# The rest columns of x of problem B, issued without a wait for the main transposing load

## The chip, the cores and the metric

The kernel runs on one core of one Trainium2 chip. The metric is device time in microseconds (us) of one execution. TensorE (PE) does the matmuls, VectorE (DVE) and ScalarE (ACT) move results out of the accumulators in PSUM, GpSimd (POOL) copies V, and SyncE (SP) does nothing but issue transfers (DMAs). ACT issues DMAs too. All transfers run on the same 16 DMA engines.

## The reference

Two independent problems, A and B, with inputs of the same shapes and no mask. Each one is a block of grouped-query attention over a given K and V cache, with the projection into Q before it and the output projection behind it. The two outputs stand side by side in the result.

```
x (16, 80, 576)   k_cache, v_cache (16, 16, 512, 128)   wq (576, 4096)   wo (4096, 576)   all bfloat16
q      = (x @ wq) as 16 x 32 heads x 80 x 128
k, v   = each of the 16 cached heads used by two query heads
p      = softmax(q k^T / sqrt(128))
out    = (p v, heads side by side) @ wo                          # 16 x 80 x 576
result = concatenate(out of A, out of B)                         # 16 x 80 x 1152
```

## The kernel before

**Units.** The work is cut into 128 units. A unit is one batch row and four cached heads: 512 keys by 128 channels for each of the four, 512 KB of K and 512 KB of V. Units 0 to 63 are problem A, units 64 to 127 problem B. Within a problem, 16 units (all batch rows) share four cached heads and so one block of 1024 columns of wq and 1024 rows of wo. Four units in a row share one block of 320 rows of x.

**What happens to a unit.** K comes from memory through a transposing DMA (`em_ldk`, L931) into `kT`, which has `NK` = 5 buffers, so unit U uses the buffer of unit U-5. The scores are matmuls of 160 columns (L898), 16 for each unit; ACT takes the exponential (L903) into `P`. V comes through a plain DMA (`em_ldv`, L935) into `v_in`; POOL copies it (L938) into `v_sb`, which has a column of ones for the row sums. P times V is L995 and L1011, the normalisation L1030 and L1035, the transposition of the result L1054, the output projection L1091. The projection of x into Q (L871) reads the transposed x in `xT` and is done in pieces between the other matmuls, some units ahead of its use.

**x.** `xT` holds the transposed x in `NX` = 5 slots of 320 rows. The 576 columns are five chunks of 128: four full ones, and a fifth made of the last 128 columns. Problem A's four blocks are loaded at the start and transposed on PE. Problem B's four blocks (numbers 4 to 7) come through transposing DMAs in the middle of the run: `em_ldx` (L807) brings columns 0 to 511 of a block, and `em_ldx2` (L810) the last 128, "the rest columns". Block 4 goes to slot 4, which was empty; blocks 5, 6 and 7 go to slots 0, 1 and 2, which held blocks of problem A. No projection of problem B reads them until it has waited for both landings.

**Order and waits.** Each operation is registered with `add(engine, key, ...)`. The key is a time in units of its own (16 for each unit); on each engine the operations are issued in the order of the keys, strictly one after the other, so an operation that waits holds up everything behind it on its engine. `_Sched.finalize` derives the waits: an operation that writes a named resource waits for its last writer and for all its readers since. The engine waits by a semaphore, and a DMA's semaphore counts when the data has landed. `xres(sl)` names the resources of problem A's block in slot `sl`; `em_ldx` lists them as written, so it waits until the last projection of A has read the slot.

**SP's queue.** SP issues all the K loads, half of the V loads (ACT has the other half), the loads of x, and nearly all stores of results (`out`, L1130). Problem B's x loads have keys that put them between K loads: block 4 ahead of the K load of unit 42, block 5 ahead of unit 52's, block 6 ahead of unit 56's, block 7 ahead of unit 60's, each with its L807 and L810 next to each other.

Of the kernel before, what the change touches and what calls it, by code (L numbers as in the profile page):

```python
# [618 lines left out]
def bass_concat_heads__gqa_block_cached__gqa_block_cached__near_ridge_kernel(  # L619
# [9 lines left out]
    B, SQ, D = A_x.shape  # L629
# [39 lines left out]
    xT = sb("xT", [128, 5, NX * QN], BF16)  # L669
# [27 lines left out]
    def R(res, ver):  # L697
        return (res, ver)
# [4 lines left out]
    def add(eng, key, emit, dur=0.0, after=None, **kw):  # L703
        op = S.add(eng, key + 1000.0, emit, **kw)
        if eng == "pe":
            pe_time.append((op, dur))
        if after is not None:
            follow.append((op, after))
        return op
# [60 lines left out]
    def xres(c):  # L770
        return [("xT", c, g, part) for g, n in XB[c] for part in range(n)]
# [29 lines left out]
    for xb in range(4, 8):  # L801
        c = xb - 4
        x_ap = probs[1][0].rearrange("b s d -> (b s) d")[c * QN:(c + 1) * QN, :]
        sl = xb % NX

        def em_ldx(e, x_ap=x_ap, sl=sl):
            return e.dma_start_transpose(xT[:, 0:4, sl * QN:(sl + 1) * QN], x_ap[:, 0:512].rearrange("n (c d) -> n c d", d=128))  # L807

        def em_ldx2(e, x_ap=x_ap, sl=sl):
            return e.dma_start_transpose(xT[:, 4, sl * QN:(sl + 1) * QN], x_ap[:, D - 128:D])  # L810

        t = 16.0 * (36, 46.5, 50, 54)[c] + 9.0
        add("sp", t, em_ldx, writes=[R(("xT", sl, "B", 0), xb)] + ([R(r_, xb) for r_ in xres(sl)] if sl < 4 else []),
            dsem="d_x%d" % sl, name="ldx%d" % xb)
        add("sp", t + 0.1, em_ldx2, writes=[R(("xT", sl, "B", 1), xb)] + ([R(r_, xb) for r_ in xres(sl)] if sl < 4 else []), dsem="d_x%d" % sl, name="ldx%db" % xb)

    for goct in range(2 * NOCT):
        prob, q = divmod(goct, NOCT)
        wq_ap, wo_ap = probs[prob][3][:, q * 1024:(q + 1) * 1024], probs[prob][4][q * 1024:(q + 1) * 1024, :]
        sl = goct % 2  # L820
        if goct == 0:
            for hf, (n0, n1) in enumerate(WQ0):
                def em_a(e, wq_ap=wq_ap, n0=n0, n1=n1):
# [3 lines left out]
                    dsem="d_wi%d" % hf, name="ldwa0.%d" % hf)  # L827
# [5 lines left out]
        else:  # L833
            for ck in range(5):
# [6 lines left out]
                if goct == 2:  # L841
                    wr += [R(("wi", hf), 1) for hf in range(4)] if ck == 0 else []
                add("act", 256.0 * (goct - 1) + 16.0 + 20.0 * ck if goct > 1 else W1_T[ck], em_w,
                    writes=wr, dsem="d_wq%d" % sl, name="ldw%d.%d" % (goct, ck))
        for pc in range(4):
            def em_wo(e, wo_ap=wo_ap, sl=sl, pc=pc):
# [3 lines left out]
            t = 256.0 * goct - 56.0 + 22.0 * pc  # L850
            add("act", t if goct else WO_T[pc], em_wo, writes=[R(("wo", sl, pc), goct)], dsem="d_wo%d" % sl,
                name="ldwo%d.%d" % (goct, pc))

    for m in range(2 * NOCT * 4):
        goct, c = divmod(m, 4)
        prob = goct // NOCT
        wsl, qsl, xb = goct % 2, m % NQ, prob * 4 + c
        xsl = xb % NX
        for i in range(8):
            g, s_ = divmod(i, 2)  # L860
            t = 64.0 * m - 88.0 + 8.0 * i + 3.3
            if m == 0:
                t = -96.0 + 2.0 * i
            if 0 < m < 8:
                t = Q_T[m - 1][0] + Q_T[m - 1][1] * i
# [57 lines left out]
    for U in range(NSU):  # L923
# [21 lines left out]
        if U < NKP:  # L945
# [8 lines left out]
            def em_ldy(e, kc_ap=kc_ap, b=b, q=q, kin=kin):  # L954
# [3 lines left out]
                name="ldy%d" % U)  # L958
# [20 lines left out]
    def tmain(W, k):  # L979
        return 64.0 * W + T_PV0 + T_PV1 * k  # L980
# [5 lines left out]
    for W in range(NW):  # L986
        for k in range(16):
# [4 lines left out]
            def em_pv(e, g=g, bank=bank, off=off, vps=vps, U=U):  # L992
# [8 lines left out]
                writes=[R(("ps", bank), ("O", F))], name="pv%d.%d" % (U, g), dur=0.228)  # L1001

        def em_pr(e, W=W):
# [15 lines left out]
            writes=[R(("ps", PVB[(7 * W + 5) % 2]), ("O", 7 * W + 5)), R(("ps", PVB[(7 * W + 6) % 2]), ("O", 7 * W + 6))],  # L1019
            name="pr%d" % W, dur=1.12)  # L1020

        for f in range(7):
# [9 lines left out]
            def em_nrm(e, bank=bank, nt=nt, c0=c0, osl=osl):  # L1032
# [7 lines left out]
                writes=[R(("o", osl), F)], name="nrm%d" % F, after=(tn, sub + 0.1, 0.0))  # L1040

        for u in range(5):
# [3 lines left out]
            t = (tmain(W, 3 * lastf + 2) if lastf < 5 else 64.0 * W + T_PR + 4.0) + (9.5 if u < 3 else 7.5) + (1.5 if u == 4 else 0.0)  # L1046
# [27 lines left out]
    for h8 in range(NH8):  # L1074
# [3 lines left out]
        for n in range(10):  # L1078
            ti, ch = divmod(n, 2)
            r = 5 * hb + ti  # L1080
            t = (128.0 * h8 + 66.0 + 12.8 * n if h8 else OP_T[0] + OP_T[1] * n)
            if h8 == NH8 - 1:
                t = 64.0 * (NW - 1) + LAST_T[n]
# [53 lines left out]
    for k, (key, _, emit, reads, name, ver, evac) in enumerate(jobs):  # L1137
        bank = JB[k % 3]
        jo = add("pe", key, lambda e, emit=emit, bank=bank: emit(e, bank), reads=reads, writes=[R(("ps", bank), ver)],
                 name=name, dur={"qp": 0.68, "op": 0.98, "tr": 0.228, "tk": 0.228, "tx": 0.28}[name[:2]])  # L1140
        for eng, ek, em, rd, wr, _d in evac:
            add(eng, 0.0, lambda e, em=em, bank=bank: em(e, bank), reads=[R(("ps", bank), ver)] + rd, writes=wr,
                name="ev_" + name, after=(jo, 0.35, 0.0))
# [33 lines left out]
    def em_c4(e):  # L1177
# [3 lines left out]
        writes=[R(("ps", 0), ("C",))], name="chk3")  # L1181
# [95 lines left out]
```

## Time and profile before

| | |
|---|---|
| median of 7 runs | 704.97 us |
| lowest and highest of them | 696.30 and 718.67 us |
| the profiled execution: its time, its span | 697.21 us, 695.4 us |
| PE, DVE, ACT, POOL busy, share of the span | 98%, 57%, 55%, 35% |
| K loads (L931), median from issue to landing | 7.7 us |
| L807 and L810, four each, median from issue to landing | 6.1 and 4.8 us |

The profiled execution is 7.8 us shorter than the median of the runs and near the shortest of them. SP and the DMA-issuing part of ACT have no busy time in the profile; their instructions are seen in the timeline, with start and length. The DMA share of a stretch is the time of all packets over the time of 16 engines; packets overlap, so it reaches 1.1 to 1.2 where the engines are full. The list of waits names, for SP, the semaphore that changed last; where SP's instructions stand end to end in the timeline, it did not wait before them.

### The profile page before, as it was taken

The numbers are of one execution on the slowest core, as the hardware profiler recorded it, in microseconds if no ns is written. First come the engines' busy times: TensorE is split into PE (matmuls) and PEld (weight loads), VectorE is DVE, ScalarE is ACT, GpSimd is POOL, SyncE is SP. The second block draws the span as 40 slices with busy tenths as digits, with TensorE's granted clock in tenths as the row PEclk, the third lists the DMA queues.
The fourth block names the chain that finished last, engine by engine and source line by source line (L and its number), as shares of the span: only waits on it lengthen the run. The fifth ranks groups of instructions, "written<-read, shape, count | busy, mean of one in ns | idle before, by whom it ended". The sixth has DMA issues, their size and how long they took to land.

```text
span 695.4 us, 21455 instructions
## 1 busy us (share of the span) xinstructions
PE 678.7 (98%) x9471; PEld 584.5 (84%) x9471; DVE 399.6 (57%) x1016; ACT 383.1 (55%) x741; POOL 242.6 (35%) x136
## 2 busy tenths in 40 slices
PE   7999999999999999999897999999999999999997
PEld 4799887888888888888786888888888888888896
DVE  3664554566666666656565445555666665666655
ACT  2388565555555555555454666665555555555561
POOL 2333434434324443323432244422344422344430
PEclk9999999999999999999999999999999999999999
DMA  9999999999999999999999999999999999998981
GB/s 285 243 237 215 225 264 265 235 209 253 258 262 228 236 245 249 230 191 236 209 286 186 263 253 262 243 256 256 198 233 227 264 208 226 238 234 208 189 188 46
DMA packets 354073, 160.60 MB, mean 231 GB/s; under 512 B 268472, under 2 KB 349880, under 8 KB 353976
## 3 DMA queue, kind: packets, MB, share of 16 engines
q1 hardware_dynamic: 310872, 112.18, 83.3%
q10 hardware_dynamic: 43104, 47.01, 23.0%
q8 instruction: 75, 1.23, 0.7%
q14 instruction: 22, 0.18, 0.1%
HBM read 89.55 MB, written 2.95 MB: 133 GB/s over the span
## 4 chain that ended last, share of the span: by engine, by line
PE 85%; DMA 6%; issue 4%; POOL 2%; DVE 1%; ACT 0%; SPq 0%; ACTq 0%; POOLq 0%
PE ps L871 22%; PE ps L1091 20%; PE ps L898 18%; PE ps L995 15%; PE ps L1011 5%; PE ps L1054 5%; DMA kT<-in_A_k_cache_dram 3%; POOL v_sb L938 2%; DMA acc<-in_A_x_dram 2%; DMA v_in<-in_A_v_cache_dram 1%; DMA v_in<-in_B_v_cache_dram 1%; PE ps L963 1%; ACT P L903 0%; ACTq L935 0%; DVE o_sb L1035 0%
## 5 line engine op out<-in xcount | busy, mean ns | idle before, releaser
L903 ACT ACTIVATE P<-ps 128x480 bf16<-128x480 f32 (+1 forms) x683 | 360.3, 571 | 257.6 <-PE ps L898 240.9
L938 POOL COPY v_sb<-v_in 128x2048 bf16<-128x2048 bf16 x128 | 239.9, 1897 | 433.6 <-PE ps L1011 260.8
L898 PE MATMUL ps<-qT,kT 128*128 128x160 bf16 x2048 | 243.8, 232 | 6.8 <-DMA kT<-in_B_k_cache_dram 3.3
L871 PE MATMUL ps<-xT,wq_sb 128*128 128x320 bf16 x1280 | 212.7, 299 | 1.7 <-DMA wq_sb<-in_A_wq_dram 1.5
L995 PE MATMUL ps<-v_sb,P 128*128 128x130 bf16 x2048 | 203.2, 221 | 0.9 <-POOL v_sb L938 0.9
L878 DVE CAST qT<-ps 128x320 bf16<-128x320 f32 x252 | 131.0, 520 | 121.6 <-PE ps L871 120.1
L898 PEld LDWEIGHTS ps<-qT,kT 128*128 128x128 bf16 x2048 | 159.3, 97 | 25.5 <-issue 6.4
L995 PEld LDWEIGHTS ps<-v_sb,P 128*128 128x128 bf16 x2048 | 147.6, 98 | 8.2 <-POOL v_sb L938 1.3
L1091 PE MATMUL ps<-wo_sb,oM 128*128 128x288 bf16 x1024 | 146.3, 286 | 0.0
L871 PEld LDWEIGHTS ps<-xT,wq_sb 128*128 128x128 bf16 x1280 | 116.9, 97 | 34.0 <-ACT xT L796 1.7
L1035 DVE TENSOR_TENSOR o_sb<-ps,rinv 128x384 bf16<-128x384 f32 (+1 forms) x224 | 120.6, 538 | 7.7
L1091 PEld LDWEIGHTS ps<-wo_sb,oM 128*128 128x128 bf16 x1024 | 96.4, 98 | 21.0
L1061 DVE COPY oM<-ps 128x512 bf16<-128x512 bf16 x128 | 54.0, 422 | 47.8 <-PE ps L1054 47.5
L1108 DVE TENSOR_TENSOR acc<-ps,acc 128x288 f32<-128x288 f32 x80 | 36.6, 458 | 47.6 <-PE ps L1091 47.6
L1054 PE MATMUL ps<-ident,o_sb 128*128 128x128 bf16 x640 | 60.0, 219 | 0.0
L1030 DVE RECIPROCAL rinv<-ps 128x3 f32<-128x3 f32 (+1 forms) x224 | 38.5, 172 | 37.1 <-PE ps L1011 26.9
L1054 PEld LDWEIGHTS ps<-ident,o_sb 128*128 128x128 bf16 x640 | 44.3, 98 | 1.6
L1011 PE MATMUL ps<-v_sb,P 128*32 128x130 bf16 x2048 | 36.5, 223 | 0.5 <-DVE o_sb L1035 0.2
L1091 PE MATMUL ps<-wo_sb,oR 128*128 128x288 bf16 x256 | 36.5, 286 | 0.0
L1011 PEld LDWEIGHTS ps<-v_sb,P 128*32 128x32 bf16 x2048 | 30.7, 98 | 5.1 <-DVE o_sb L1035 1.3
L1113 DVE TENSOR_TENSOR osb<-ps,acc 128x288 bf16<-128x288 f32 x40 | 18.3, 457 | 20.9 <-PE ps L1091 20.9
L1103 ACT COPY acc<-ps 128x288 f32<-128x288 f32 x40 | 16.0, 400 | 23.9 <-PE ps L1091 23.6
(33 smaller groups left out, 83.2 us busy)
## 6 DMA issues: line engine op xcount, KB each, us to landing
v_in<-in_A_v_cache_dram SPq DMA_DIRECT2D x42, 512.0 KB, 5.5
v_in<-in_B_v_cache_dram ACTq DMA_DIRECT2D x32, 512.0 KB, 5.3
v_in<-in_B_v_cache_dram SPq DMA_DIRECT2D x32, 512.0 KB, 5.2
v_in<-in_A_v_cache_dram ACTq DMA_DIRECT2D x22, 512.0 KB, 5.8
wo_sb<-in_A_wo_dram ACTq DMA_DIRECT2D x16, 288.0 KB, 4.6
wo_sb<-in_B_wo_dram ACTq DMA_DIRECT2D x16, 288.0 KB, 4.7
wq_sb<-in_B_wq_dram ACTq DMA_DIRECT2D x16, 256.0 KB, 4.8
wq_sb<-in_A_wq_dram ACTq DMA_DIRECT2D x13, 256.0 KB, 6.3
```

The costliest lines, as they stand in the source:

```text
L871: last = e.matmul(ps[:, bank, 0:QN], lhsT=wq_sb[:, wsl, ck, i * 128:(i + 1) * 128], rhs=xT[:, ck, xsl * QN:(xsl + 1) * QN], start=(ck == 0 ...
L878: return e.copy(dst, src) if ev == "act" else e.tensor_copy(dst, src)
L898: last = e.matmul(ps[:, sbk, c * 160:(c + 1) * 160], lhsT=kT[:, U % NK, j, g * 128:(g + 1) * 128], rhs=qT[:, (U // 4) % NQ, U % 4, g, :], ...
L903: return e.activation(P[:, psl, 0:k, :], ps[:, sbk, 0:k * 160].rearrange("p (c n) -> p c n", c=k), AF.Exp, scale=SCALE)
L938: return e.tensor_copy(v_sb[:, vps, :, 0:128], v_in[:, vs, :, :].rearrange("p g (j d) -> p (g j) d", j=4))
L995: last = e.matmul(ps[:, bank, off:off + OP_], lhsT=pap(16 * U + 4 * g + j, 0, 128), rhs=v_sb[:, vps, 4 * g + j, :], start=(j == 0), stop=( ...
L1011: last = e.matmul(ps[32 * g:32 * g + 32, bank, off:off + OP_], lhsT=pap(16 * U + 4 * g + j, 128, 160), rhs=v_sb[:, U % NVP, 4 * g + j, :], ...
L1030: return e.reciprocal(rinv[:, c0:c0 + nt], ps[:, bank, 128:128 + OP_ * (nt - 1) + 1:OP_])
L1035: return e.tensor_tensor(o_sb[:, osl, 0:nt, :], src, sc, AluOpType.mult)
L1054: last = e.transpose(psb[:, bank, 128 * n_:128 * n_ + 128], o_sb[:, F % NOF, pos, :], ident[:])
L1061: return e.tensor_copy(oM[:, osl2, :, 128 * b8:128 * b8 + 128], psb[:, bank, 0:512].rearrange("p (g c) -> p g c", g=4))
L1091: last = e.matmul(ps[:, bank, 0:DC], lhsT=w, rhs=wo_sb[:, wsl, i, ch * DC:(ch + 1) * DC], start=(i == 0), stop=(i == 7))
```

## The change

`em_ldx2` no longer lists the resources of problem A's block as written. It had two effects there: a wait for readers, which `em_ldx` just ahead of it on SP has already done, and, since `em_ldx` had become their last writer, a wait for the landing of `em_ldx`'s DMA. Both are gone for blocks 5, 6 and 7; block 4 had neither. The instructions, their number and their order on every engine stay as they were; in SP's list, three waits on the semaphores of `xT` are the whole difference.

```
@@ -812,7 +812,7 @@
         t = 16.0 * (36, 46.5, 50, 54)[c] + 9.0
         add("sp", t, em_ldx, writes=[R(("xT", sl, "B", 0), xb)] + ([R(r_, xb) for r_ in xres(sl)] if sl < 4 else []),
             dsem="d_x%d" % sl, name="ldx%d" % xb)
-        add("sp", t + 0.1, em_ldx2, writes=[R(("xT", sl, "B", 1), xb)] + ([R(r_, xb) for r_ in xres(sl)] if sl < 4 else []), dsem="d_x%d" % sl, name="ldx%db" % xb)
+        add("sp", t + 0.1, em_ldx2, writes=[R(("xT", sl, "B", 1), xb)], dsem="d_x%d" % sl, name="ldx%db" % xb)
```

## The prediction

> **What bounds the kernel now.** First the page's line of busy times: PE is busy in 98% of the span, so whatever is gained must come out of PE's idle time.
>
> ```profile
> PE 678.7 (98%) x9471; PEld 584.5 (84%) x9471; DVE 399.6 (57%) x1016; ACT 383.1 (55%) x741; POOL 242.6 (35%) x136
> ```
>
> Next the busy time by stretch (the first figure is the stretch's length, the second PE's busy time; the last two are DMA share and GB/s). PE has no idle time from 200 to 300 us, none from 405 to 660, and loses 0.77 us and 5.25 us in the two stretches between: 6.0 us, at an unthrottled clock.
>
> ```profile
> 200.00:300.00 100.00, 100.00 (x1415) 86.71 (x1413) 61.74 (x157) 54.66 (x104) 35.56 (x19) 1.00 1.12 236
> 300.00:345.00 45.00, 44.23 (x611) 37.94 (x608) 27.26 (x68) 23.75 (x45) 15.05 (x8) 1.00 1.07 219
> 345.00:385.00 40.00, 34.75 (x502) 29.85 (x503) 20.88 (x55) 18.95 (x36) 11.32 (x6) 1.00 1.17 242
> ```
>
> The list of PE's waits says for whom: the score matmuls wait for the landing of K. These 5.5 us are nearly all of the 6.0.
>
> ```profile
> PE ps L898 <- DMA kT<-in_B_k_cache_dram: 3.3, 1, 3.3
> PE ps L898 <- DMA kT<-in_A_k_cache_dram: 2.2, 2, 2.0
> ```
>
> Why is K late? SP's list of waits holds the three that the change removes, and SP's timeline shows them as holes ahead of L810:
>
> ```profile
> SPq L810 <- DMA xT<-in_B_x_dram: 12.4, 3, 5.3
> ```
>
> ```profile
> 214.78 2.55 SPq L807 DMA_TRANSPOSE xT<-in_B_x_dram  x1
> 217.38 1.24 SPq L810 DMA_TRANSPOSE xT<-in_B_x_dram  x1
> 218.67 4.81 SPq L931 DMA_TRANSPOSE kT<-in_A_k_cache_dram  x1
> ...
> 264.55 1.40 SPq L807 DMA_TRANSPOSE xT<-in_B_x_dram  x1
> 270.00 1.14 SPq L810 DMA_TRANSPOSE xT<-in_B_x_dram  x1
> 271.18 2.35 SPq L931 DMA_TRANSPOSE kT<-in_A_k_cache_dram  x1
> ...
> 291.43 1.39 SPq L807 DMA_TRANSPOSE xT<-in_B_x_dram  x1
> 298.15 1.58 SPq L810 DMA_TRANSPOSE xT<-in_B_x_dram  x1
> 299.78 3.32 SPq L931 DMA_TRANSPOSE kT<-in_A_k_cache_dram  x1
> ...
> 316.71 1.41 SPq L807 DMA_TRANSPOSE xT<-in_B_x_dram  x1
> 321.17 1.14 SPq L810 DMA_TRANSPOSE xT<-in_B_x_dram  x1
> ...
> 323.63 2.00 SPq L931 DMA_TRANSPOSE kT<-in_A_k_cache_dram  x1
> ```
>
> Block 4 (214.78) has no hole: it shows already what the other three will look like. Blocks 5, 6 and 7 have holes of 4.05, 5.33 and 3.05 us. I counted the score matmuls, 16 for each unit, to get the end of the last one that reads each K buffer, and compared it with the start of the next K load into that buffer. Unit 51's load starts 0.1 us after its buffer is free (260.5); unit 56's, behind block 6, 13.7 us after; unit 60's, behind block 7, 16.4 us after; unit 68's still 12.4 us; only at unit 82 (431 us) is it back to 2.1. In all that time SP's instructions stand end to end: the queue is behind and can't catch up quickly. Counted the other way, K lands 13.3 us before its first use for unit 51, and 0.3, 0.2, 0.1 and 0.3 us before it for units 56, 61, 63 and 68. The stalls of 2.0 and 3.3 us are at units 63 and 68. So the place of the three waits is ahead of every one of these stalls.
>
> **The change part by part.** *Added or moved:* no instruction. SP's list differs by three waits alone, so that the edit does nothing is excluded. *Removed:* waits of 12.4 us on SP. Queued behind each are a K load, a V load and, at block 7, two stores. *Whom the wait served:* nobody. The projections of problem B that read blocks 5 to 7 wait for both landings themselves; block 7 lands at 324.5 us, and the first projection that needs it is due some 70 us later by its key and the times of the units around it (block 6's some 65 us after its landing, block 5's some 75), so x itself has cover to spare.
>
> *How much of the 12.4 us SP really gets back.* This the trace doesn't show directly, so I bound it. A load of x is followed by a K load; I take the time from the start of L807 to the end of that K load's issue. With a wait: 8.98 (block 5), 11.67 (block 6) and 8.92 less two stores of 1.27, so 7.65 (block 7), together 28.3. Without: block 4's 8.70, three times 26.1. By this row the gain is only 2.2 us, because after a wait the queue of transfers has drained and the next K load is issued in 2.0 to 3.3 us, where block 4's took 4.81: SP is slowed by the DMA engines anyway. That is the lower end. The upper end is the whole 12.4.
>
> Between them stands what the DMA engines lost. If they are the limit, only the time in which they ran dry is lost. The stretches around the holes (DMA share next to last):
>
> ```profile
> 268.50:270.50 2.00, 2.00 (x75) 1.64 (x72) 1.01 (x2) 1.38 (x3) 0.00 (x0) 1.00 1.09 353
> 270.50:273.00 2.50, 2.50 (x37) 2.04 (x26) 2.02 (x6) 0.71 (x2) 2.28 (x2) 1.00 0.35 81
> ...
> 297.50:300.50 3.00, 3.00 (x36) 2.56 (x34) 1.54 (x5) 2.49 (x5) 1.37 (x1) 1.00 0.52 128
> ...
> 320.70:322.20 1.50, 1.50 (x14) 1.16 (x12) 0.72 (x2) 0.69 (x2) 0.00 (x0) 1.00 0.14 23
> ...
> 324.00:325.00 1.00, 1.00 (x15) 0.92 (x14) 0.84 (x2) 0.47 (x2) 0.00 (x0) 1.00 0.42 91
> ```
>
> In the first 2 us after SP stopped issuing, ACT's transfers filled the engines (share 1.09). Then they ran dry. Against a full share of 1.10 the loss is 2.5 x (1 - 0.35/1.10) = 1.70, then 1.58, 1.31 and 0.62: 5.2 us. I take this value: it is measured at the resource that limits SP, and it lies between the two ends.
>
> The Trainium skill, page "DMA: Bandwidth & Descriptors", section "Issuing engines are not separate DMA queues", speaks against the change: transfers issued from several engines run on the same 16 DMA engines and interleave, so a pause on SP would cost nothing while ACT has work, and the sum by it would be 0. The row at 268.50 agrees for 2 us, the row at 270.50 doesn't. The same page's section "Anatomy of one DMA" gives about 2.0 us fixed for a DMA on GpSimd's path, most of it the receipt of the last write, and its "Specifications" 0.6 us to the first byte on SP's path; an estimate from these figures would be 3 x 2.6 = 7.8 us.
>
> *Where the stall goes.* An earlier SP shifts all K loads from unit 52 on. 1.70 + 1.58 of the relief is there before the first stall (307 us), all of it before those of 2.0 and 3.3 us. PE's idle time of 6.0 us then falls to about 0.8, and 6.0 is also the most that can be gained in this execution. The sum in its own time: 697.2 - 5.2 = 692.0 us. The median of the runs is 7.8 us longer, by losses that this trace can't show; I subtract the same 5.2 from it: 699.8 us. What is late next would be V: POOL's copy for unit 62 ends 1.3 us before its first use, and unit 66's 2.6 us. V loads follow the K loads in SP's queue and come earlier too.
>
> **The rivals.** *A: the gain is over 1% (7 us).* The longer runs may lose their additional 7.8 us in the same place: K landing with 0.1 to 0.3 us to spare leaves no reserve when a transfer is slow, and unit 68's K took 11.5 us to land against a median of 7.7. Then the stall of the median run is up to 6.0 + 7.8 = 13.8 and the change takes up to 12.4 of it: 692.6 us. For it: the thin margins and the spread of 22 us between runs. Against it: the same spread may come from anywhere, and the relief is 12.4 only if SP and not the DMA engines sets the pace.
>
> *B: hidden anyway.* Block 4's row is the truth, the relief is 2.2 us or less: 702.8 to 705.0. For it: the DMA share is 1.07 to 1.17 throughout. Against: the dry rows.
>
> *C: slower.* Three transposing loads in a row make the third crawl. The next K load's issue took 2.35, 3.32 and 2.00 us after a wait, 2.56 on average. The worst K load of the trace, in a spell of slow transfers, took
>
> ```profile
> 368.09 9.00 SPq L931 DMA_TRANSPOSE kT<-in_B_k_cache_dram  x1
> ```
>
> With that behind each block the cost is 3 x (9.00 - 2.56) = 19.3 against the 12.4 gained: SP 6.9 us later, all of it on PE, 711.9 us. It decides when the issue behind a pair takes over 2.56 + 12.4/3 = 6.7 us. For it: block 4's stretch from 219 to 223 moved only 194 GB/s at a share of 1.46. Against it: block 4's own K load took 4.81.
>
> **How the numbers follow.** Forecast (gain of 2.2 to 7) 0.40; A 0.38; B 0.10; C 0.12, a quarter of it within 1%. A measurement of this kernel can tell about 1% from no change. So faster 0.38; same 0.40 + 0.10 + 0.03 = 0.53; slower 0.09. The likeliest case gives 699.8. The range, 692 to 708, goes from A's end to halfway into C, since the median of a few runs spread over 22 us moves by itself. The forecast's own range is 698 to 703.
>
> **What would show it.** Right: SP's timeline has no hole between L807 and L810 at blocks 5 to 7; the DMA share shows no dry stretch there; unit 60's K load starts about 11 us after its buffer is free, not 16; PE's waits for `kT` fall from 5.5 us to under 1. Wrong: K loads behind the pairs issued in over 6.7 us (C); PE's idle time from 300 to 405 us still near 6 with the holes gone (B); PE's idle time gone and the time still the same, which would mean that runs differ by something else.

## The result, and the profile after

The changed kernel ran in 699.48 us (median of 23 runs, 688.20 to 715.33), the kernel before, run beside it, in 703.17 us (median of 60, 696.30 to 720.31). The ratio is 0.9908, with a 95% interval from 0.9875 to 0.9940; each ratio in this text leaves out the runs of a kernel that lie over 1.5% above its fastest, which keeps 8 of these 23 runs and 43 of these 60. Over all runs the mean is 4.4 us shorter (95%, by resampling the runs, as for all means below: 1.8 to 7.0). The profiled execution took 693.26 us, with a span of 691.4 us (before: 697.21 and 695.4).

Busy times on the page hardly move: the work is the same.

```profile
PE 679.1 (98%) x9471; PEld 585.1 (85%) x9471; DVE 400.2 (58%) x1016; ACT 382.5 (55%) x741; POOL 242.5 (35%) x136
```

SP's timeline after (start, length, line) at blocks 5, 6 and 7:

```profile
267.32 1.40 SPq L807 DMA_TRANSPOSE xT<-in_B_x_dram  x1
268.76 1.25 SPq L810 DMA_TRANSPOSE xT<-in_B_x_dram  x1
270.06 2.62 SPq L931 DMA_TRANSPOSE kT<-in_A_k_cache_dram  x1
...
287.04 3.02 SPq L807 DMA_TRANSPOSE xT<-in_B_x_dram  x1
290.10 1.25 SPq L810 DMA_TRANSPOSE xT<-in_B_x_dram  x1
291.39 4.69 SPq L931 DMA_TRANSPOSE kT<-in_A_k_cache_dram  x1
...
310.24 1.42 SPq L807 DMA_TRANSPOSE xT<-in_B_x_dram  x1
311.70 2.00 SPq L810 DMA_TRANSPOSE xT<-in_B_x_dram  x1
313.75 1.23 SPq L1130 DMA_DIRECT2D out_dram<-osb  x2
315.02 2.95 SPq L931 DMA_TRANSPOSE kT<-in_A_k_cache_dram  x1
```

The three holes are gone; each L810 starts within 0.06 us of L807's end. The DMA engines no longer run dry there (DMA share next to last, GB/s last; in the third row they are busy, but move only 107 GB/s):

```profile
270.00:273.00 3.00, 3.00 (x79) 2.50 (x68) 1.95 (x7) 0.95 (x2) 2.09 (x2) 1.00 1.21 288
...
290.50:292.00 1.50, 1.50 (x70) 1.34 (x71) 0.70 (x3) 0.71 (x3) 0.36 (x1) 1.00 1.23 307
...
313.00:315.00 2.00, 2.00 (x24) 1.67 (x22) 1.57 (x5) 0.72 (x3) 2.00 (x2) 1.00 1.34 107
```

What PE makes of it, by stretch (length, PE's busy time, ...):

```profile
300.00:345.00 45.00, 45.00 (x625) 38.98 (x623) 27.84 (x70) 24.31 (x47) 15.09 (x9) 1.00 1.14 232
345.00:385.00 40.00, 39.47 (x556) 33.77 (x554) 23.59 (x62) 21.33 (x41) 11.71 (x7) 1.00 1.13 226
385.00:405.00 20.00, 18.07 (x261) 15.42 (x260) 9.10 (x24) 11.08 (x23) 9.22 (x6) 1.00 1.11 246
```

PE's idle time from 200 to 405 us falls from 6.1 to 2.5 us: the 0.77 us before 345 is gone, the 5.25 us up to 385 is down to 0.53 us, and 1.93 us stands in the last stretch, where there was 0.11. The span is 4.0 us shorter. The list of PE's waits names what is left, K again:

```profile
PE ps L898 <- DMA kT<-in_B_k_cache_dram: 2.5, 3, 1.1
...
PE ps L898 <- DMA kT<-in_A_k_cache_dram: 0.3, 1, 0.3
```

The 2.5 us are in the middle of the run; the 0.3 us stand at 135 us, ahead of the change.

Set against the counts of the prediction (how long after its buffer is free a K load starts, called its lateness below): unit 56's load starts 5.1 us late and not 13.7, unit 60's 8.0 and not 16.4, unit 64's 5.1 and not 13.5. Then SP loses it again: unit 68's load is 11.1 us late and unit 72's 16.0 (before 12.4 and 12.7). The waits that are left, of 0.53 us at 369.8, 0.81 at 387.0 and 1.12 at 393.3, are in that second stretch.

### The profile page after: what moved, and what is told of

Its sections match the earlier page's. It is cut to its first block, busy times and chain, and to the rows that moved or that the text cites. A ratio compares the mean times of both kernels' runs of the same rounds, so it can differ in the third digit from the quotient of the medians.

```text
span 691.4 us, 21455 instructions
## 1 busy us (share of the span) xinstructions
PE 679.1 (98%) x9471; PEld 585.1 (85%) x9471; DVE 400.2 (58%) x1016; ACT 382.5 (55%) x741; POOL 242.5 (35%) x136
## 3 DMA queue, kind: packets, MB, share of 16 engines
HBM read 89.55 MB, written 2.95 MB: 134 GB/s over the span
## 4 chain that ended last, share of the span: by engine, by line
PE 90%; DMA 8%; DVE 0%; SPq 0%; issue 0%; ACT 0%
PE ps L871 23%; PE ps L1091 22%; PE ps L898 19%; PE ps L995 16%; PE ps L1011 5%; PE ps L1054 5%; DMA kT<-in_B_k_cache_dram 4%; DMA acc<-in_A_x_dram 2%; DMA wo_sb<-in_A_wo_dram 2%; DMA kT<-in_A_k_cache_dram 1%; PE ps L963 0%; DVE o_sb L1035 0%; PE ps L788 0%; SPq L777 0%; DVE osb L1113 0%
## 5 line engine op out<-in xcount | busy, mean ns | idle before, releaser
L1113 DVE TENSOR_TENSOR osb<-ps,acc 128x288 bf16<-128x288 f32 x40 | 18.3, 457 | 20.9 <-PE ps L1091 20.9
```

## The experiments

Theory S (SP's lateness): what counts is how late SP issues K for units 52 to 68, where K has no reserve; holes on SP there cost PE time, holes elsewhere don't. Rival D: time in which the DMA engines run dry costs wherever it falls. Rival X: the gain belongs to the loads of x themselves, or to the two transposing loads being side by side.

A K load can be made to wait for the landing of the K load before it without touching x. This edit to the changed kernel does that for chosen units:

```
-            add("sp", t_k, em_ldk, writes=[R(("kT", ks, j), U) for j in range(4)], dsem="d_k%d" % ks, name="ldk%d" % U)
+            add("sp", t_k, em_ldk, reads=[R(("kT", (U - 1) % NK, 0), U - 1)] if U in (54, 58, 62) else [], writes=[R(("kT", ks, j), U) for j in range(4)], dsem="d_k%d" % ks, name="ldk%d" % U)
```

**Three holes in the middle** (h_mid3: units 54, 58 and 62).

> The changed kernel, with three new holes in SP's queue that have nothing to do with x: the K loads of units 54, 58 and 62 wait for the landing of the K load just ahead of them. Theory S (a hole in SP's queue between 260 and 400 us makes K late, and PE waits): three holes of 3 to 6 us there, so about 4 to 7 us of the gain goes back, time near the kernel before (ratio to before 0.996 to 1.004), and PE waits for kT for 4 us or more. Rival X (the gain has to do with x's own loads): ratio stays near 0.991, PE's waits for kT stay near 2.8 us. Rival D (time lost on the DMA engines costs the same wherever it is lost) expects here the same as S.

Measured: median 704.81 us (12 runs) beside 703.42 us of the kernel before (29 runs); ratio 0.9923 (0.9875 to 0.9971). That is below the 0.996 to 1.004 that theory S gave and close to rival X's 0.991. Over all runs the mean difference to the kernel before is 0.1 us (-3.6 to 3.7), as theory S has it. The profile has the holes on SP and more waiting on PE than before the change (waits that stand alone are listed at L1209, the line that issues them):

```profile
SPq L1209 <- DMA kT<-in_A_k_cache_dram: 11.2, 3, 8.3
```

```profile
PE ps L898 <- DMA kT<-in_A_k_cache_dram: 7.6, 5, 2.8
PE ps L898 <- DMA kT<-in_B_k_cache_dram: 3.4, 1, 3.4
```

Three holes with no part in the loads of x take 11.2 us from SP. Of PE's 11.0 us, 2.4 are at 136 and 142 us, ahead of the holes; the 8.6 in the middle stand against 5.5 before the change. Ratio and mean point different ways: three holes alone don't decide between S and X.

**Six holes in the middle** (h_mid6: units 50, 54, 58, 62, 66 and 70).

> The same with six holes, at the K loads of units 50, 54, 58, 62, 66 and 70 (some 255 to 375 us). Theory S: the first is swallowed by the reserve, the other five cost 2 to 5 us each, so 10 to 25 us more than the changed kernel, ratio to before 1.005 to 1.027. Rival X: 0.991. Rival D: the same as S.

Measured: median 709.59 us (12 runs), ratio 1.0060 (1.0016 to 1.0105): slower than before the change, within theory S's 1.005 to 1.027 and far from rival X's 0.991. The mean over all runs is 5.0 us longer than before (1.6 to 8.5). In the profile PE waits 10.8 us for K, all of it from 307 to 396 us:

```profile
PE ps L898 <- DMA kT<-in_B_k_cache_dram: 8.4, 4, 3.8
PE ps L898 <- DMA kT<-in_A_k_cache_dram: 2.4, 2, 1.7
```

**The same six, late in the run** (h_late6: units 86, 90, 94, 98, 102 and 106, whose K loads fall between 445 and 555 us in the profile before, and between 470 and 576 us in this run's own).

> The same six holes where SP is not late: at the K loads of units 86, 90, 94, 98, 102 and 106 (some 445 to 555 us), where K lands 8 to 14 us before its use. Theory S: nothing is lost, the ratio to before stays at 0.988 to 0.994, and PE has no idle time from 405 to 660 us. Rival D: 10 to 25 us more, as in the middle.

Measured: median 702.49 us (12 runs), ratio 0.9954 (0.9914 to 0.9995). The ratio is above the 0.988 to 0.994 that theory S gave, though its interval overlaps with the changed kernel's. The trace decides what the holes did. Its profiled execution, at 711.33 us the longest of the twelve, waits for K ahead of the holes only, at 231 us and from 311 to 410 us:

```profile
PE ps L898 <- DMA kT<-in_B_k_cache_dram: 9.4, 5, 4.2
PE ps L898 <- DMA kT<-in_A_k_cache_dram: 4.5, 2, 2.5
```

That is 13.9 us, where the changed kernel's profile has 2.8; up to there the two have the same instructions. So the waits in one profile move by 11 us between executions, and the waits of h_mid3 and h_mid6 above are by themselves no measure of what their holes cost. The holes here are larger than h_mid6's (13.1 + 4.2 us):

```profile
SPq L1209 <- DMA kT<-in_B_k_cache_dram: 25.3, 6, 6.6
```

```profile
445.00:555.00 110.00, 110.00 (x1532) 95.44 (x1530) 64.75 (x165) 62.79 (x122) 38.37 (x21) 1.00 1.03 234
555.00:660.00 105.00, 105.00 (x1474) 91.03 (x1472) 64.89 (x162) 56.72 (x107) 37.44 (x20) 1.00 1.07 233
```

25.3 us of waiting on SP, and PE without a gap through it and behind it. K loads start at most 7.3 us late there and, where the landing is in the trace, K lands 6.7 us or more before its use. Against h_mid6, on the same chip and with the same number of holes, the mean over all runs is 7.3 us shorter (3.2 to 11.3), and the intervals of the two ratios lie apart. So the place decides and not the hole: rival D falls. Rival X falls with h_mid6, where holes at K loads alone cost the gain and more.

**One wait kept** (keep6: of the three, only block 6's stays).

```
-        add("sp", t + 0.1, em_ldx2, writes=[R(("xT", sl, "B", 1), xb)], dsem="d_x%d" % sl, name="ldx%db" % xb)
+        add("sp", t + 0.1, em_ldx2, writes=[R(("xT", sl, "B", 1), xb)] + ([R(r_, xb) for r_ in xres(sl)] if xb == 6 else []), dsem="d_x%d" % sl, name="ldx%db" % xb)
```

> The changed kernel with one of the three waits kept, the longest one (block 6, 5.33 us in the profile before). By the time in which the DMA engines ran dry it is worth 1.6 of 5.2 us, so 699.5 + 1.1 to 1.6 us, ratio to before 0.992 to 0.994; by SP's time it is worth 5.33 of 12.43, so 0.994 to 0.996. If the three together do something that no single one does (a threshold): near 1.000. The first two are closer than the interval will be wide; the profile should show unit 60's K load 10 to 13 us behind, between 8 and 16.

Measured: median 701.30 us (12 runs) beside 705.59 us (23 runs), ratio 0.9903 (0.9844 to 0.9962). The changed kernel, run again with it (after_again), gave 702.19 us and 0.9885 (0.9820 to 0.9950). The two can't be told apart: one wait is too small for this measurement. In its profile that wait is 2.5 us and unit 60's load 8.2 us late, less than the 10 to 13 expected. PE has no wait for K from 300 to 385 us, and one of 4.9 us at 398 us, for unit 71. It says nothing on whether the three add up evenly.

**The changed kernel again** (after_again).

> The changed kernel once more, beside the next three on the same chip, so that they can be compared with it and not with the kernel before alone. Ratio to before 0.9875 to 0.994 as measured. A second profile of it: if its 2.5 us of waits for K at units 68 to 72 were chance, they are gone or elsewhere; if the place is given by the schedule, K is late again at units 65 to 73.

Median and ratio are given above. Its profile repeats the place of what is left: K lands 0.2 to 0.5 us before its use at units 68, 71, 72 and 73, and PE waits 2.8 us for unit 68's at 372 us:

```profile
PE ps L898 <- DMA kT<-in_B_k_cache_dram: 2.8, 1, 2.8
```

So the second loss comes back in the same place; unit 68 is also the one for which PE waited 3.3 us before the change. In this execution unit 60's load starts 11.8 us late and unit 64's 8.8, where the first profile had 8.0 and 5.1. What stands at the second loss on SP, in the timeline of the changed kernel's first profile:

```profile
358.49 1.22 SPq L1130 DMA_DIRECT2D out_dram<-osb  x2
359.75 2.19 SPq L931 DMA_TRANSPOSE kT<-in_B_k_cache_dram  x1
362.08 1.28 SPq L935 DMA_DIRECT2D v_in<-in_B_v_cache_dram  x1
363.42 9.00 SPq L931 DMA_TRANSPOSE kT<-in_B_k_cache_dram  x1
372.46 1.24 SPq L1130 DMA_DIRECT2D out_dram<-osb  x2
373.74 4.37 SPq L931 DMA_TRANSPOSE kT<-in_B_k_cache_dram  x1
...
378.83 6.00 SPq L931 DMA_TRANSPOSE kT<-in_B_k_cache_dram  x1
384.88 1.22 SPq L1130 DMA_DIRECT2D out_dram<-osb  x2
```

Stores of problem A (0.6 us each), and a K load of unit 69 that takes 9.00 us to issue there and in the profile before (7.66 in after_again), while ACT loads wq for problem B. The next three runs try both.

**Stores of A from ACT** (st_act):

```
-                    se = "act" if last and ti == 3 and pi else "sp"
+                    se = "act" if prob == 0 or last and ti == 3 and pi else "sp"
```

> The changed kernel, with the stores of problem A's results (20 of them, 0.6 us each on SP between 305 and 391 us) issued by ACT instead of SP. SP gets 12.5 us back in the stretch where it is still late (16.0 us behind at unit 72). If the issuing on SP sets the pace: PE's remaining 2.5 us of waits for kT at 370 to 393 us go, 2 to 5 us less than the changed kernel, ratio to before 0.984 to 0.988. If the 16 DMA engines set the pace and SP is only held up by them: no gain, 0.990 to 0.993, and K loads on SP take as much longer as the stores have freed. If ACT's exponentials are held up by the stores: slower than the changed kernel, with PE waiting for P.

Measured: median 699.72 us (6 runs) beside 703.42 us, ratio 0.9896 (0.9835 to 0.9957): not to be told from the changed kernel. Unit 72's load is 4.9 us late and not 16.0, as wanted, but K still lands 0.2 to 0.4 us ahead of use at units 65 to 67, and PE waits 3.2 us at 373 us. The K loads of units 66 and 67 take 7.7 and 8.6 us to issue, as in the second of the expected cases.

**That block of wq later** (wq_late: the five loads of wq for the second block of heads of problem B move by 36 in the key):

```
-                add("act", 256.0 * (goct - 1) + 16.0 + 20.0 * ck if goct > 1 else W1_T[ck], em_w,
+                add("act", 256.0 * (goct - 1) + (52.0 if goct == 5 else 16.0) + 20.0 * ck if goct > 1 else W1_T[ck], em_w,
```

> The changed kernel, with the five loads of the next block of wq on ACT's queue (363 to 392 us in the profile before, 360 to 392 after) some 12 us later. They share the stretch with V, stores and the late K loads: unit 69's K load took 9.00 us to issue there in both profiles. If that crowding is what makes K late at units 68 to 72: K load issues there stay under 6 us, PE's 2.5 us of waits for K go, ratio to before 0.984 to 0.989. If the crowding is there with or without wq: 0.990 to 0.993, a K load issue of 8 to 9 us near 360 us still.

Measured: median 697.89 us (6 runs) beside 705.59 us, ratio 0.9894 (0.9802 to 0.9986). The first of the two expected cases fails in the trace: K loads of 7.32 and 9.27 us are still there (units 69 and 71), and PE waits 6.8 us for K. The loads of wq alone don't make the slow K loads.

**Both** (st_act_wq, and the same kernel again beside its counterpart as st_act_wq2).

> Both together: problem A's stores from ACT, and the block of wq later. If SP's issuing and the crowding each have a share: PE without waits for K from 200 to 405 us, ratio to before 0.980 to 0.987, better than the changed kernel. If the DMA engines alone limit: as wq_late. If ACT is held up by the stores: PE waits for P, 0.990 or more.

> The version with problem A's stores from ACT and the block of wq 12 us later, once more, beside the same version with the three waits put back. If its first result was not chance: 693 to 698 us median, ratio to before 0.980 to 0.990, and K margins over 4 us at units 56 to 73.

Measured: medians 694.44 us (6 runs, beside 705.59) and 692.71 us (12 runs, beside 702.35), ratios 0.9882 (0.9797 to 0.9967) and 0.9881 (0.9837 to 0.9925). The medians are 11.2 and 9.6 us below those of the kernel before, against the change's own 3.7 us. Beside the changed kernel on the same chip (after_again) the first is 5.4 us shorter in the mean over all runs (0.5 to 10.2), but the ratios of the two, 0.9882 and 0.9885, can't be told apart: that this version beats the kernel before is shown, that it beats the changed kernel is likely. In the first profile PE has no wait for K behind 152 us (one of 3.2 us there, of 0.35 us at 138). In the second no K load from unit 61 on starts over 6.8 us late, K lands at least 5.2 us before use in the whole middle, and PE has not a single wait for K in the run:

```profile
300.00:345.00 45.00, 45.00 (x629) 39.15 (x628) 27.85 (x69) 25.01 (x47) 16.84 (x9) 1.00 1.18 254
345.00:385.00 40.00, 40.00 (x567) 34.66 (x565) 24.22 (x64) 22.57 (x45) 14.46 (x8) 1.00 1.20 243
385.00:405.00 20.00, 20.00 (x287) 17.39 (x286) 9.87 (x26) 12.19 (x26) 7.97 (x5) 1.00 1.13 263
```

**The three waits put back into that version** (waits_back): with the second loss removed, the change by itself.

```
-        add("sp", t + 0.1, em_ldx2, writes=[R(("xT", sl, "B", 1), xb)], dsem="d_x%d" % sl, name="ldx%db" % xb)
+        add("sp", t + 0.1, em_ldx2, writes=[R(("xT", sl, "B", 1), xb)] + ([R(r_, xb) for r_ in xres(sl)] if sl < 4 else []), dsem="d_x%d" % sl, name="ldx%db" % xb)
```

> That version with the three waits of the kernel before put back. Theory S: the waits make SP 7 to 10 us later from unit 60 on, and K's margin at units 57 to 61, 4.5 us in the profile without them, is used up: PE waits 1 to 5 us for K near 310 to 345 us, but SP recovers by unit 68, since neither stores nor wq hold it up there. So the waits cost less than in the kernel before: 0 to 5 us. If the waits cost by themselves and not by SP's lateness: the whole 6 us again.

Measured: median 700.15 us (12 runs) beside 692.71 without the waits, on the same chip; ratio to the kernel before 0.9960 (0.9910 to 1.0010) beside 0.9881. Over all runs the waits cost 5.5 us of mean (1.9 to 9.0), 7.4 of median: above theory S's 0 to 5 and near the 6 of the other case (the waits cost by themselves), and the interval holds both. SP's list of waits, its timeline, and PE's list:

```profile
SPq L810 <- DMA xT<-in_B_x_dram: 13.5, 3, 5.2
```

```profile
269.02 1.41 SPq L807 DMA_TRANSPOSE xT<-in_B_x_dram  x1
274.58 1.14 SPq L810 DMA_TRANSPOSE xT<-in_B_x_dram  x1
...
294.66 1.40 SPq L807 DMA_TRANSPOSE xT<-in_B_x_dram  x1
301.31 1.14 SPq L810 DMA_TRANSPOSE xT<-in_B_x_dram  x1
...
322.65 1.42 SPq L807 DMA_TRANSPOSE xT<-in_B_x_dram  x1
328.20 1.13 SPq L810 DMA_TRANSPOSE xT<-in_B_x_dram  x1
```

```profile
PE ps L898 <- DMA kT<-in_A_k_cache_dram: 5.8, 4, 2.8
PE ps L898 <- DMA kT<-in_B_k_cache_dram: 1.7, 2, 1.4
```

The holes are back (4.2, 5.3 and 4.1 us), unit 56's load starts 12.1 us late and unit 60's 18.1 (5.3 and 8.0 without the waits). K lands 0.1 to 1.1 us before its use at units 56, 57 and 61, and PE waits 1.86 and 0.40 us for it at 318.6 and 336.1 us. Not all of the difference between these two profiled executions (spans of 699.9 and 686.8 us) belongs to the waits: 3.5 us of the 5.8 is at 138 and 145 us, before any of them. And SP had not recovered by unit 68 (11.1 us late), as it should have by the expectation; PE's last 1.7 us of waits for K, at 395 and 401 us, are behind that. Lateness handed on past unit 68 is a reason for a cost above 5 us that the trace shows; what each wait cost is not measured.

## Why the prediction was right, and where it missed

**The time, the sign and the path were right**: 699.8 us against 699.48, in the forecast's own range. That the two agree to 0.3 us is partly luck: the median of 7 runs from which 5.2 us was taken lay 1.8 us above the 703.17 measured beside the change, and the medians differ by 3.7 us and not 5.2. SP's lateness, K without reserve, PE's waits for it, and the three waits ahead of them are one chain: it was lengthened (h_mid6), cut off from its end (h_late6) and put back (waits_back). "Whom the wait served: nobody" holds: no wait of PE for x came up in its place.

**What SP gets back was somewhat too small.** The term is "5.2 us", the time in which the DMA engines ran dry. The prediction's own rows, from the start of L807 to the end of the next K issue, give after the change 5.36 (block 5), 9.04 (block 6) and 7.73 less two stores of 1.27, so 6.46 (block 7): 20.9 against 28.3, a gain of 7.4. In the changed kernel's second profile the gain is 6.7. How much of it reaches unit 60 is not settled: its lateness is 8.0 us in one profile and 11.8 in the other (16.4 before), so "about 11 us after its buffer is free" agrees with the second. The low end of 2.2 rested on block 4's 8.70; the same instructions took 5.22 and 9.28 in the two profiles after, so this row alone moves by 4 us between executions, and three times one row was no bound. The dry time counts the engines' loss against a share of 1.10; with the 1.21 to 1.34 of these stretches after the change the same rows give 5.5 us, so the choice of the share explains little of the gap. One row is misplaced: "the first 2 us after SP stopped issuing" begin at 268.50, 2.5 us after the end of L807's issue.

**"PE's waits for `kT` fall from 5.5 us to under 1" was wrong**: in the middle they fell to 2.5, and PE's idle time by 3.7 and not 5.2. The step that failed is "What is late next would be V". It is K again: SP arrives early at units 64 to 66 and then loses its lead, over unit 67 and the next five, to the stores and to slow K loads. In the second profile even the stall at unit 68, which the relief should have covered, is still 2.8 us of 3.3. The trace of before showed the parts of it (the load of 9.00 us and unit 68's lateness of 12.4), but the relief was carried on as if nothing behind it could use it up. With the stores and wq out of the way no wait for K is left in the middle, in two profiles out of two.

**The argument against the change**, that a pause on SP costs nothing, was the prediction's own inference from the Trainium skill, page "DMA: Bandwidth & Descriptors", section "Issuing engines are not separate DMA queues", which says that transfers of all issuing engines interleave on the same 16 DMA engines. The inference holds late in the run, where 25.3 us of pauses on SP cost PE nothing. In the middle the measurement decides against it: 13.5 us of pauses cost 5.5 us of mean.

**The two misses cancel in part.** A relief that was larger by the rows met a second loss. Which part of the median's 3.7 us is which can't be read from medians with intervals of this width.

**Rival A** (over 1%): its 692.6 us was not reached, but the ratio's interval, 0.60 to 1.25% faster, spans the border. Its mechanism, that longer runs lose time at the same place, has support in the last section. **Rival B** falls: by the rows the relief is 7.4 and 6.7 us and not 2.2. **Rival C**: the K loads behind the pairs were issued in 2.62, 4.69 and 2.95 us (2.93, 5.55 and 2.14 in the second profile), none over its deciding 6.7.

## What to carry to other kernels

A wait on an engine that only issues transfers is priced by two things: how late that queue already is where its next customer has no reserve, and what stands behind in the queue to use up what is given back. Six holes cost 7.3 us more of mean in the middle than late in the run, where K had some 7 us to spare. Count, for each buffer, when it is free, when its load starts, when it lands and when it is read, before and behind the edit: the next place with a reserve near zero is the next bound, and here moving two more things away from it took the median some 10 us below the kernel before, against the change's 3.7.

## What the runs showed of the hardware

**A short wait of PE may cost half-clock time behind it.** In h_mid6 the 3.76 us wait at 396 us ends in a stretch with a granted clock of one half; this is that stretch by itself (clock third from last):

```profile
396.13 0.56 PE L898 MATMUL ps<-qT,kT 128*128 128x160 bf16 x3 [3.76 <-DMA kT<-in_B_k_cache_dram]
```

```profile
395.60:399.00 3.40, 2.87 (x19) 2.31 (x20) 0.85 (x3) 1.14 (x2) 0.00 (x0) 0.50 1.27 215
```

The record lasts 3.4 us; PE works 2.87 us of it at half clock, so about 1.4 us is lost on top of the wait (an estimate), and it adds to a late K what no list of waits shows. The same record follows waits of 3.4 us (h_mid3, at 381), 2.8 and 1.9 us (waits_back, at 138 and 319) and 2.8 us (after_again, at 372). It does not follow waits of 3.3 us (before, at 375), 3.5 us (wq_late, at 374) and 3.2 us (st_act_wq, at 152). The Trainium skill, page "TensorE: Matmul & The Clock Gate", section "Part 1: The HAM clock gate", has a gate of two states, half and full, judged over free-running windows of about 3.4 us. The values 0.50 and 3.4 us agree, and the traces show such windows: cut each trace into stretches of 3.41 us, on the grid on which its own clock records begin. Between the first 20 and the last 15 us of the twelve traces, twelve stretches at full clock are followed by half clock, and in each of them PE was busy for 0.2 to 1.55 us; no stretch at full clock with over 1.6 us of work is followed by it, and of those with 1.4 to 1.6 us some are. Before's wait of 3.3 us falls across two stretches, with 1.77 and 1.78 us of work; the 1.9 us of waits_back fall into one, which had 1.55 us left. By these counts the part of one window that a wait takes decides, and not its length alone.

This bears on the 7.8 us between the median and the profile of before, which the prediction left as losses that the trace can't show. Neither profile, before or after, has such a record ahead of its last 2 us. Over 25 executions of the changed kernel time and mean granted clock go together (correlation -0.86): 688 to 697 us at 0.998 or 0.999 for the five shortest, 698 to 706 at 0.990 to 0.997 for the next nineteen, 715 at 0.987 for the longest. Lost clock is the smaller part of it: what is missing to 1, times the span, is about 3.5 us at 0.995 and 9 at 0.987 (an estimate). The waits for K grow too: three profiles of the changed kernel's instructions up to 445 us (after, after_again, h_late6) have 2.8, 3.3 and 13.9 us of them in executions of 693.26, 695.32 and 711.33 us. That the long runs of the kernel before lose their time there as well is likely, but no profile of one was taken.

**The same issue takes very different times.** Block 4's pair and the K load behind it, the same instructions in both kernels, took 8.70 us in one execution and 5.22 and 9.28 in two others. Differences of that size in a single profile are no evidence for an edit of this size.
